# One more fold for the rows n of 2 mod 4 in sequences 1 to 7 of a fused Fourier-mixing and squared-ReLU kernel

## The chip, the cores and the metric

The kernel runs on one core of a Trainium2 chip. The metric is the device time of one execution in microseconds (us). The core's engines work beside each other and meet through semaphores: TensorE (PE in the profile, with its weight loads as PEld), VectorE (DVE), ScalarE (ACT), GpSimd (POOL) and SyncE (SP), which issues most DMA transfers. A group of 128 rows of on-chip memory is called 128 partitions; matmul results land in PSUM, everything else in SBUF.

## What is computed

```python
X = np.fft.fft(np.fft.fft(x, axis=1), axis=2).real   # x: (8, 3008, 256), float32
h = X.reshape(24064, 256) @ w_in                     # w_in: (256, 2048)
out = np.maximum(h, 0.0) ** 2 @ w_out                # w_out: (2048, 256)
```

So eight sequences of S = 3008 rows go through a two-dimensional Fourier transform, of which the real part is kept, and then through two dense layers with a squared ReLU between them. All of it is in float32.

## The kernel before

**The transform along the sequence.** The rows of x come to the kernel in groups of four: n, S - n, S/2 - n and S/2 + n, for n from 0 to S/4 = 752. Sums and differences of the four (the folds, on VectorE) leave two kinds of folded rows, kp = 0 and kp = 1, which feed the outputs k of even and of odd number. What is left is a product of a cosine or sine table with the folded rows. The rows n are split into classes, because a table row of an even n repeats itself with changed signs in the second half of its columns, and so needs only half of them:

- class 0: n of 0 mod 8, one tile of 95 rows, a quarter of the columns (94 or 95)
- class 1: n of 4 mod 8, one tile of 94 rows, 94 or 95 columns
- class 2: n of 2 mod 4 (the rows of the title), two tiles of 96 and 92 rows, half of the columns (188 or 189)
- class 3: the odd n, three tiles of 128, 128 and 120 rows, all columns (376 or 377)

The seven tiles are numbered t = 0 to 6, in this order: tiles 2 and 3 are class 2, and `ODD0` is tile 4.

For sequences 1 to 7 the odd rows (class 3) already get one fold more, n against S/4 - n. Tile 5 is loaded in reversed blocks of 32 rows, `f_turn` (L423; shuffle at L427 or L430, copy f0 at L433) reverses each block in turn, `f_even` (L443) makes the sum and the difference for kp = 0, `f_sine` (L448) multiplies by a sine on ScalarE, and `f_odd` (L452) combines by a cosine for kp = 1. Then `odd_n` (L549) needs half the columns for each product, 188 or 189, at L565. For kp = 1 the cosine and the sine part come out apart, side by side; ScalarE copies one to SBUF ("oc", L569) and `join_odd` (L572) adds and subtracts them into the columns of even and odd number. `part_table` (L325) sorts the columns of the tables of class 3 in place, once, before sequence 1.

**The groups of the transform.** Each sequence has four groups: `which` (0 for P, from the cosine tables, 1 for Q, from the sine tables) times kp. A group is five pieces: `even_n` (L494: four products, one each of classes 0 and 1 and two of class 2, through `product` at L475, whose matmul is at L487; then a copy on ScalarE, L502), `join_4`, `join_2`, `odd_n` and `join_1`. For kp = 1 `join_odd` comes between the last two. The joins run on VectorE. The even and odd products write to a ring of two PSUM buffers (psd).

**The dense layers.** A sequence is cut into six blocks of 251 (or 250) columns k, each block into eight steps j. A step has a `front` (L631) in two halves h: two products into PSUM buffer "ph" (L641, L642; a ring of two, so half h of a step needs what half h of the step before used), three VectorE operations that read it (L644, L646, L647), and after each half a call of `between`. ScalarE then applies ReLU and square (L656, L657), GpSimd makes four sums (L664 to L667), and two steps later `back` does seven products (L694). `gather` (L711 to L728) and the two transposing `store` parts (L758, L759) follow each block.

**What sets the order.** The engines run what the program emits, in that order. The folds and the transform of sequence b + 1 are done during the dense layers of sequence b. `ahead` (L766) lists them as pieces, each with a written weight, and `between` hands pieces out: each call lowers `spent` by `pace` (all weights over the number of calls, 78 in a sequence, 53 in the first), and pieces are emitted while `spent` is at or below zero, each raising it by its weight. After a tile of the odd class its `f_odd` is held back and put at the fourth place among the next tile's pieces. Sequence 0 is transformed ahead of all dense work, by the same helpers but without the further fold.

Of the kernel before, what the change touches and what calls it, by code (L numbers as in the profile page):

```python
# [8 lines left out]
F32 = mybir.dt.float32  # L9
# [4 lines left out]
P = 128  # L14
R = 32
# [67 lines left out]
def kernel(  # L83
# [12 lines left out]
    nc = tc.nc  # L96
    B, NROW, _, D = x.shape
    S = out.shape[0] // B
# [9 lines left out]
    TILES = class_tiles(S)  # L108
    NT = len(TILES)
    NC = column_counts(S)  # L110
    PLACE, WT = table_places(S)
# [3 lines left out]
    const = ctx.enter_context(tc.tile_pool(name="const", bufs=1))  # L115
    xp = ctx.enter_context(tc.tile_pool(name="xp", bufs=NX))
# [3 lines left out]
    hp = ctx.enter_context(tc.tile_pool(name="hp", bufs=3))  # L120
# [3 lines left out]
    op = ctx.enter_context(tc.tile_pool(name="op", bufs=2))  # L124
# [9 lines left out]
    xt = {}  # L134
# [3 lines left out]
    ODD0 = NT - 3  # L138
    HALF = S // 16
    REST = HALF - P  # L140
# [2 lines left out]
           [(0, P, H // 2)] + [(H // 2 + p, 2 * HALF - P - p - R, R) for p in range(0, H // 2, R)]]  # L143
    assert H == P and REST <= H // 2 and TILES[ODD0][0] == 3 and TILES[ODD0 + 1][1] == TILES[ODD0][1] + P

    def load_x(b, t):
        c, r0, step, rows = TILES[t]
        if b and c == 3:
            xt[b, t] = xp.tile([P, 4, D], F32, name="xt", tag="x")
            for p, first, count in ODD[t - ODD0]:  # L150
                nc.sync.dma_start(out=xt[b, t][p:p + count], in_=x[b, S // 8 + 1 + first:S // 8 + 1 + first + count])
            return

        while rows % 15 and rows % 16 and r0 + step * rows < NROW:
            rows += 1

        pool, tag = (gp, "g") if b == 0 and t < NT - NX else (xp, "x")
        xt[b, t] = pool.tile([P, 4, D], F32, name="xt", tag=tag)
        nc.sync.dma_start(out=xt[b, t][0:rows], in_=x[b, r0:r0 + step * (rows - 1) + 1:step])
# [3 lines left out]
    cosT = const.tile([P, 2, WT], F32, name="cosT")  # L163
# [147 lines left out]
    PQE = {}  # L311
    PART = (slice(0, H + 1), slice(H + 1, D))
    REVERSE = list(range(R - 1, -1, -1))
    turn = const.tile([P, 3, 2], F32, name="turn")

    def make_turn():
        for i in range(2):
            for a, tab in enumerate((cosT, sinT, sinT)):
                nc.scalar.mul(turn[:, a, i:i + 1], tab[:, 1, PLACE[ODD0 + i]:PLACE[ODD0 + i] + 1], -1.0 if a == 2 else 1.0)

    rows_used = const.tile([P, 1], F32, name="rows_used")
    nc.vector.memset(rows_used, 0.0)
    nc.vector.memset(rows_used[0:REST], 1.0)

    def part_table(tab, i):  # L325


        nk, at = NC[0][3], PLACE[ODD0 + i]
        v = tab[:, 0, at:at + nk]
        a = op.tile([P, nk], F32, name="tp", tag="os")  # L330
        nc.scalar.mul(a, v, rows_used if i else 1.0)
        nc.scalar.copy(v[:, 0:(nk + 1) // 2], a[:, 0::2])
        nc.scalar.copy(v[:, (nk + 1) // 2:], a[:, 1::2])

    def columns(tab, t, part):

        nk, at = NC[0][3], PLACE[t]
        nq = (nk + 1) // 2
        return tab[:, 0, at + part * nq:at + (nk if part else nq)]

# [21 lines left out]
    def fold(b, t):  # L362


        odd = b > 0 and t >= ODD0
        r = slice(0, P if odd else TILES[t][3])
        st = {}

        def new(pool, nm, shape):
# [30 lines left out]
        def w_of(t):  # L400
            if (b, t) not in folded:
                folded[b, t] = wp.tile([P, 2, D], F32, name="w", tag="w")
            return folded[b, t]
# [9 lines left out]
        if b == 0:  # L413
            return [f_s, f_d, f_sc, f_dc, lambda: (f_w(PART[0]), f_e()), lambda: f_w(PART[1])]
        ops = [(0.9, f_s), (0.9, f_d), (0.7, f_sc), (0.6, f_dc), (1.1, f_w)]
        if not odd or t == ODD0:
            return ops, None


        i = t - ODD0 - 1  # L420
        rows = slice(0, TILES[ODD0 + i][3] if i == 0 else REST)

        def f_turn():  # L423
            w = w_of(t)
            if i == 0:
                st["v"], st["w"] = w_of(ODD0), w
                nc.vector.stream_shuffle(w, w, REVERSE)  # L427
            else:
                st["v"], st["w"] = w, w_of(NT)
                nc.vector.stream_shuffle(st["w"][0:H // 2], w[H // 2:P], REVERSE)  # L430
                nc.gpsimd.memset(st["w"][H // 2:P], 0.0)
            spare("f0", "f0")
            nc.scalar.copy(st["f0"][rows], st["v"][rows, 0])  # L433
# [21 lines left out]
                nc.vector.scalar_tensor_tensor(out=u, in0=u, scalar=turn[rows, 0, i:i + 1], in1=st[nm][rows],  # L455
                                               op0=ALU.mult, op1=ALU.add)

        return ops + [(0.8, f_turn), (1.3, f_even), (0.2, f_sine)], (1.4, f_odd)

    def dft_ops(b):  # L460

# [6 lines left out]
        def group(kp, which):  # L468
# [6 lines left out]
            def product(ps, c, lone_e=False, only=None):  # L475

                ts = [t for t in range(NT) if TILES[t][0] == c]
                for t in ts if only is None else ts[only:only + 1]:
                    rows = TILES[t][3]
                    if b is None:  # L480
                        w = we[0:rows, kp, t, 0:n]
                    elif lone_e:
                        w = lone[0:rows, 2 * t + kp]
                    else:
                        w = folded[b, t][0:rows, kp, PART[which]]
                        w = w if which else w[:, 0:n]
                    nc.tensor.matmul(ps[0:w.shape[-1]], w,  # L487
                                     (cosT if lone_e else tab)[0:rows, kp, PLACE[t]:PLACE[t] + NC[kp][c]],
                                     start=t == ts[0] and (lone_e or not both_in), stop=t == ts[-1] and not lone_e,
                                     skip_group_check=both_in)  # L490
# [3 lines left out]
            def even_n():  # L494
                st["ps"] = psd.tile([P, 512], F32, name="pd", tag="d")[0:n]
                for c, at, nk in EVEN:
                    product(st["ps"][:, at:at + nk], c)
                copy_4()

            def copy_4():  # L500
# [36 lines left out]
            def join_2():  # L537
                a, ps = st["b"], st["ps"]
                st["c"] = hp.tile([P, NC[0][3]], F32, name="dc2", tag="dc2", bufs=2)[0:n, 0:n0]
                both(st["c"][:, 0:n1], st["c"][:, n1:n0], a, ps[:, 2 * n2:2 * n2 + n1])  # L540

            def odd_part(i, lone_e):

# [2 lines left out]
                    st["odd"] = pool.tile([P, 512], F32, name="pd", tag=tag)[:, 0:n0]  # L546
                product(st["odd"], 3, lone_e, i)

            def odd_n():  # L549
                ps = psd.tile([P, 512], F32, name="pd", tag="d")[0:n]  # L550
                st["odd"] = ps[:, 0:n0]
                if b is None:
                    return product(ps[:, 0:n0], 3)
                nq = (n0 + 2) // 2 if kp else (n0 + 1) // 2
                for part in range(2):
                    if kp:
                        tab, o = (cosT, sinT)[part], 0
                        to = ps[:, part * nq:part * nq + nq]
                        other = part != which
                    else:  # L560
                        tab, o = (cosT, sinT)[which], part
                        to = ps[:, part:n0:2]
                        other = part != which
                    for i, pair in enumerate(((ODD0, ODD0 + 1), (ODD0 + 2, NT))):
                        nc.tensor.matmul(to, folded[b, pair[other]][:, kp, PART[which]][:, 0:n],  # L565
                                         columns(tab, ODD0 + i, o), start=i == 0, stop=i == 1)
                if kp:
                    st["cos"] = hp.tile([P, nq], F32, name="oc", tag="oc", bufs=1)[0:n]
                    nc.scalar.copy(st["cos"], ps[:, 0:nq])  # L569
                    st["sin"] = ps[:, nq:2 * nq]  # L570

            def join_odd():  # L572

                a, ps = st["cos"], st["sin"]
                nq = a.shape[-1]
                st["odd"] = o = hp.tile([P, NC[1][3]], F32, name="do", tag="do", bufs=1)[0:n, 0:n0]
                tt(out=o[:, 0::2], in0=a[:, 0:nq - 1], in1=ps[:, 0:nq - 1], op=ALU.add)
                if which == 1:
                    tt(out=o[:, 1::2], in0=ps[:, 1:nq], in1=a[:, 1:nq], op=ALU.subtract)
                else:  # L580
                    tt(out=o[:, 1::2], in0=a[:, 1:nq], in1=ps[:, 1:nq], op=ALU.subtract)
# [19 lines left out]
                return [((which, kp, nm), f) for nm, f in named]  # L601
            ops = [(0.1, even_n), (0.4, join_4), (0.5, join_2), (0.1, odd_n), (0.8, join_1)]
            if b and kp:
                ops.insert(4, (0.5, join_odd))
            return ops

        ops = [] if b is None else [(0.0, start)]
# [158 lines left out]
    def ahead(b):  # L766
        start, *groups = dft_ops(b)
        if b == 1:

            tables = [(0.3, lambda tab=tab, i=i: part_table(tab, i)) for i in range(2) for tab in (cosT, sinT)]  # L770
            groups = [(1.5, fold_columns)] + dft_ops(None) + tables + groups
        groups.insert(0, start)

        pieces = []
        for ops, last in [fold(b, t) for t in range(NT)] + [(groups + [(0.0, lambda: load_e(b))], None)]:
            if held:
                ops.insert(3, held.pop())
            if last:
                held.append(last)
            pieces += ops  # L780
        return pieces
# [231 lines left out]
```

## Time and profile before

The median of three runs is 1944.14 us (1943.55 to 1944.79).

| engine | busy us | share of the span | instructions |
|---|---|---|---|
| PE (matmul) | 1930.5 | 99% | 9266 |
| PEld (weight load) | 1716.5 | 88% | 9266 |
| DVE | 1396.0 | 72% | 3432 |
| ACT | 924.9 | 48% | 1074 |
| POOL | 1172.9 | 60% | 1708 |

Busy time is the time in which an engine has at least one instruction under way. One float32 product shows as two matmul records, each with its own weight load. The durations of matmul records overlap (a record of 251 columns is shown as 375 ns, while the next starts 0.21 us after it), so what a product costs TensorE is read from the chain of waits, which shows start to start: 0.42 us for the two records of a product of 251 columns. The transform of sequences 1 to 7 is a small part of TensorE's time: in the chain L487 has 1.9% and L565 1.8%, while the four dense lines L641, L642 and L694 have nearly all the rest.

### The profile page before, as it was taken

Reading aid. Unit: us, or ns where it says so; the run is one execution under the profiler, and the core shown is the slowest. Engines: PE = TensorE matmul, PEld = TensorE weight load, DVE = VectorE, ACT = ScalarE, POOL = GpSimd, SP = SyncE. Lnnn points to the kernel's source line nnn. Section 1 sums busy time; section 2 is a strip of 40 time slices with the busy share of each in tenths; the row PEclk is TensorE's granted clock in tenths of the full one; section 3 lists DMA queues with packets and bytes.
Section 4 is the critical chain, followed back from the end, with each engine's and each line's share of the span. In section 5 each row is a group of like instructions: output and inputs, shape, how many; then the busy total and the mean of one; then the engine's idle time right before and its main releaser. Section 6 shows DMA issues by size and latency. Waiting matters only on the chain.

```text
span 1942.7 us, 27736 instructions
## 1 busy us (share of the span) xinstructions
PE 1930.5 (99%) x9266; PEld 1716.5 (88%) x9266; DVE 1396.0 (72%) x3432; ACT 924.9 (48%) x1074; POOL 1172.9 (60%) x1708
## 2 busy tenths in 40 slices
PE   9999999999999999999999999999999999999998
PEld 7888888888988899888988889888898888988887
DVE  8998866777677766777667776777766777655554
ACT  2854544544444444445444454444544454444443
POOL 0047646676567655766666665667656676556655
PEclk9999999999999999999999999999999999999999
DMA  7332101111111101121012100121012101100101
GB/s 216 114 36 53 38 10 49 33 31 27 27 41 32 37 12 30 39 41 28 11 35 43 40 20 12 41 48 28 20 17 52 33 12 22 27 12 12 22 11 22
DMA packets 145563, 69.55 MB, mean 36 GB/s; under 512 B 129090, under 2 KB 136204, under 8 KB 145419
## 3 DMA queue, kind: packets, MB, share of 16 engines
q1 hardware_dynamic: 144960, 66.86, 15.8%
q8 instruction: 73, 1.20, 0.3%
q14 instruction: 71, 0.58, 0.1%
q0 software_dynamic: 176, 0.65, 0.1%
q10 hardware_dynamic: 283, 0.26, 0.0%
HBM read 43.03 MB, written 24.69 MB: 35 GB/s over the span
## 4 chain that ended last, share of the span: by engine, by line
PE 95%; DVE 3%; DMA 1%; SPq 0%; issue 0%; ACT 0%; DVEq 0%
PE ph L642 17%; PE ph L641 16%; PE mC L694 16%; PE mA L694 16%; PE mB L694 16%; PE mD L694 8%; PE pd L487 2%; PE pd L565 2%; DMA raw<-in_moe_w_in_dram 1%; DVE m L263 0%; DMA xt<-in_x_dram 0%; DMA sind<-in_sin_d_dram 0%; DVE fd L261 0%; DVE he L644 0%; PE mA L681 0%
## 5 line engine op out<-in xcount | busy, mean ns | idle before, releaser
L656 ACT ACTIVATE g<-g 128x1004 f32<-128x1004 f32 (+1 forms) x384 | 399.3, 1040 | 792.5 <-DVE g L647 438.5
L644 DVE SCALAR_TENSOR_TENSOR he<-Et,gE,ph 128x251 f32<-128x251 f32 (+1 forms) x768 | 361.8, 471 | 412.5 <-PE ph L642 410.4
L664 POOL TENSOR_TENSOR s<-g 128x251 f32<-128x251 f32 (+1 forms) x376 | 246.4, 655 | 659.7 <-ACT g L657 584.7
L642 PE MATMUL ph<-Qt,G 127*128 127x251 f32 (+1 forms) x1536 | 451.9, 375 | 0.0
L641 PE MATMUL ph<-Pt,G 128*128 128x251 f32 (+1 forms) x1536 | 451.7, 375 | 0.0
L657 ACT ACTIVATE g<-g 128x1004 f32<-128x1004 f32 (+1 forms) x384 | 399.3, 1040 | 12.2
L694 PE MATMUL mC<-s,wsum 128*128 128x251 f32 (+1 forms) x1504 | 381.7, 375 | 0.0
L694 PE MATMUL mA<-g,wout 128*128 128x251 f32 (+1 forms) x1504 | 379.8, 374 | 0.0
L646 DVE TENSOR_TENSOR g<-he,ph 128x251 f32<-128x251 f32 (+1 forms) x768 | 320.5, 417 | 55.3 <-POOL s L664 1.4
L642 PEld LDWEIGHTS ph<-Qt,G 127*128 127x128 f32 x1536 | 291.5, 190 | 35.9
L641 PEld LDWEIGHTS ph<-Pt,G 128*128 128x128 f32 x1536 | 287.6, 189 | 35.5 <-DVE g L647 1.2
L694 PEld LDWEIGHTS mC<-s,wsum 128*128 128x128 f32 x1504 | 285.6, 190 | 34.7
L694 PEld LDWEIGHTS mA<-g,wout 128*128 128x128 f32 x1504 | 282.9, 189 | 36.0 <-issue 1.3
L647 DVE TENSOR_TENSOR g<-he,ph 128x251 f32<-128x251 f32 (+1 forms) x768 | 314.2, 409 | 0.0
L666 POOL TENSOR_TENSOR s<-g 128x251 f32<-128x251 f32 (+1 forms) x376 | 304.4, 810 | 0.0
L665 POOL TENSOR_TENSOR s<-s,g 128x251 f32<-128x251 f32 (+1 forms) x376 | 274.6, 730 | 29.5
L667 POOL TENSOR_TENSOR s<-g,s 128x251 f32<-128x251 f32 (+1 forms) x376 | 253.9, 675 | 0.0
L694 PE MATMUL mB<-g,wsum 128*128 128x251 f32 (+1 forms) x752 | 220.5, 374 | 0.0
L694 PE MATMUL mD<-s,wout 128*128 128x251 f32 (+1 forms) x752 | 220.3, 374 | 0.0
L694 PE MATMUL mB<-s,wout 128*128 128x251 f32 (+1 forms) x752 | 219.9, 374 | 0.0
L694 PEld LDWEIGHTS mB<-g,wsum 128*128 128x128 f32 x752 | 142.6, 190 | 17.4
L694 PEld LDWEIGHTS mD<-s,wout 128*128 128x128 f32 x752 | 141.9, 189 | 17.7
(136 smaller groups left out, 1304.4 us busy)
## 6 DMA issues: line engine op xcount, KB each, us to landing
out_dram<-os SPq DMA_DIRECT2D x376, 56.0 KB
xt<-in_x_dram SPq DMA_DIRECT2D x32, 384.0 KB
xt<-in_x_dram SPq DMA_DIRECT2D x42, 128.0 KB
Et<-e_dram SPq DMA_DIRECT2D x7, 752.5 KB
xt<-in_x_dram SPq DMA_DIRECT2D x9, 512.0 KB
out_dram<-os SPq DMA_DIRECT2D x288, 6.8 KB
raw<-in_moe_w_in_dram SPq DMA_DIRECT2D x16, 256.0 KB
raw<-in_moe_w_out_dram SPq DMA_DIRECT2D x16, 256.0 KB
```

Of the source, the lines that this page charges most:

```text
L641: nc.tensor.matmul(hP, G1[:, fs], pt[:, ks], start=True, stop=True)
L642: nc.tensor.matmul(hQ, G2[0:P - 1, fs], qt[0:P - 1, ks], start=True, stop=True)
L644: nc.vector.scalar_tensor_tensor(out=t, in0=et[:, ks], scalar=gE[:, fc:fc + 1], in1=hP, op0=ALU.mult, op1=ALU.add)
L646: tt(out=g[:, h, 0, 0:n], in0=t, in1=hQ, op=ALU.add)
L647: tt(out=g[:, h, 1, 0:n][:, ::-1], in0=t, in1=hQ, op=ALU.subtract)
L656: act(v, v, AF.Relu)
L657: act(v, v, AF.Square)
L664: gt(out=s1, in0=g21, in1=g22, op=ALU.add)
L665: gt(out=s2, in0=s1, in1=g11, op=ALU.subtract)
L666: gt(out=s3, in0=g11, in1=g21, op=ALU.subtract)
L667: gt(out=s4, in0=g12, in1=s2, op=ALU.subtract)
L694: nc.tensor.matmul(acc[nm][:, i, 0:n], w, v[:, 0:n], start=j == 0 and i == 0, stop=j == NJ - 1, skip_group_check=True)
```

## The change

In sequences 1 to 7 class 2 gets the further fold that class 3 already has. Its 188 rows are paired, first with last, so that 94 pairs are left; for each of these a sum and a difference are kept, each for half of the columns. The purpose is to stream fewer columns through TensorE: `even_n` still has two products of class 2 in each group, of 94 rows in place of 96 and 92, and of 94 or 95 columns in place of 188 or 189.

For that, tile 3 is loaded in three reversed blocks of 32 rows, and it gets the pieces turn, even, sine and odd, with weights of 0.8, 0.7, 0.2 and 1.2. `even_n` calls the new helper `once_more`, which holds what `odd_n` did before, and for kp = 1 a second `join_odd`, named "half" and weighted 0.4, comes ahead of `join_2`. It shares the buffers "oc" and "do" with the join of class 3. The tables of tile 2 are sorted as those of class 3 are, ahead of them, and `make_turn` takes three more columns of the tables.

The core of the diff:

```diff
+    TWO = ODD0 - 2
+    HALF2 = S // 32
+    ROWS2 = TILES[TWO][3]
...
+        if b and t == TWO + 1:
+            xt[b, t] = xp.tile([P, 4, D], F32, name="xt", tag="x")
+            for p in range(0, ROWS2, R):
+                at = TILES[TWO][1] + step * (2 * HALF2 - p - R)
+                nc.sync.dma_start(out=xt[b, t][p:p + R], in_=x[b, at:at + step * (R - 1) + 1:step])
+            return
...
-        odd = b > 0 and t >= ODD0
-        r = slice(0, P if odd else TILES[t][3])
+        odd, two = b > 0 and t >= ODD0, b > 0 and t == TWO + 1
+        r = slice(0, P if odd else ROWS2 if two else TILES[t][3])
...
-        i = t - ODD0 - 1
-        rows = slice(0, TILES[ODD0 + i][3] if i == 0 else REST)
+        i = 2 if two else t - ODD0 - 1
+        rows = slice(0, (P, REST, HALF2)[i])
...
-        return ops + [(0.8, f_turn), (1.3, f_even), (0.2, f_sine)], (1.4, f_odd)
+        return ops + [(0.8, f_turn), (1.3 if odd else 0.7, f_even), (0.2, f_sine)], (1.4 if odd else 1.2, f_odd)
...
                 for c, at, nk in EVEN:
-                    product(st["ps"][:, at:at + nk], c)
+                    if b and c == 2:
+                        st["half"] = once_more(st["ps"][:, at:], c, nk)
+                    else:
+                        product(st["ps"][:, at:at + nk], c)
                 copy_4()
...
-                both(st["c"][:, 0:n1], st["c"][:, n1:n0], a, ps[:, 2 * n2:2 * n2 + n1])
+                both(st["c"][:, 0:n1], st["c"][:, n1:n0], a, st["half"] if b else ps[:, 2 * n2:2 * n2 + n1])
...
+            def once_more(ps, c, nk):
+
+                nq = (nk + 2) // 2 if kp else (nk + 1) // 2
+                pairs, rows = ((((TWO, TWO + 1),), HALF2), (((ODD0, ODD0 + 1), (ODD0 + 2, NT)), P))[c == 3]
+                for part in range(2):
+                    if kp:
+                        tab, o = (cosT, sinT)[part], 0
+                        to = ps[:, part * nq:part * nq + nq]
+                    else:
+                        tab, o = (cosT, sinT)[which], part
+                        to = ps[:, part:nk:2]
+                    for i, pair in enumerate(pairs):
+                        nc.tensor.matmul(to, folded[b, pair[part != which]][0:rows, kp, PART[which]][:, 0:n],
+                                         columns(tab, pairs[0][i] if c == 3 else TWO, o)[0:rows],
+                                         start=i == 0, stop=i == len(pairs) - 1)
+                if not kp:
+                    return ps[:, 0:nk]
+                a = hp.tile([P, NC[0][3] // 2 + 1], F32, name="oc", tag="oc", bufs=1)[0:n, 0:nq]
+                nc.scalar.copy(a, ps[:, 0:nq])
+                return a, ps[:, nq:2 * nq]
...
             if b and kp:
-                ops.insert(4, (0.5, join_odd))
+                ops.insert(4, (0.5, lambda: join_odd("odd", n0)))
+                ops.insert(2, (0.4, lambda: join_odd("half", n1)))
...
-            tables = [(0.3, lambda tab=tab, i=i: part_table(tab, i)) for i in range(2) for tab in (cosT, sinT)]
+            tables = [(0.3, lambda tab=tab, t=t: part_table(tab, t)) for t in (TWO, ODD0, ODD0 + 1)
+                      for tab in (cosT, sinT)]
```

More of the change, by code (lines that the diff above doesn't have):

```diff
@@ L144 @@
     assert H == P and REST <= H // 2 and TILES[ODD0][0] == 3 and TILES[ODD0 + 1][1] == TILES[ODD0][1] + P
+    TWO = ODD0 - 2
+    HALF2 = S // 32
+    ROWS2 = TILES[TWO][3]
+    assert TILES[TWO][0] == TILES[TWO + 1][0] == 2 and HALF2 <= ROWS2 < HALF2 + R and ROWS2 % R == 0
     def load_x(b, t):
@@ L313 @@
     REVERSE = list(range(R - 1, -1, -1))
-    turn = const.tile([P, 3, 2], F32, name="turn")
+    turn = const.tile([P, 3, 3], F32, name="turn")
     def make_turn():
-        for i in range(2):
+        for i, t in enumerate((ODD0, ODD0 + 1, TWO)):
             for a, tab in enumerate((cosT, sinT, sinT)):
-                nc.scalar.mul(turn[:, a, i:i + 1], tab[:, 1, PLACE[ODD0 + i]:PLACE[ODD0 + i] + 1], -1.0 if a == 2 else 1.0)
+                r = slice(0, TILES[t][3])
+                nc.scalar.mul(turn[r, a, i:i + 1], tab[r, 1, PLACE[t]:PLACE[t] + 1], -1.0 if a == 2 else 1.0)
     rows_used = const.tile([P, 1], F32, name="rows_used")
@@ L323, with part_table @@
     nc.vector.memset(rows_used[0:REST], 1.0)
[L325 to L331, printed above, removed]
+    def part_table(tab, t):
+        nk, at = NC[0][TILES[t][0]], PLACE[t]
+        rows = TILES[t][3]
+        v = tab[0:rows, 0, at:at + nk]
+        a = op.tile([P, nk], F32, name="tp", tag="os")[0:rows]
+        nc.scalar.mul(a, v, rows_used if t == ODD0 + 1 else 1.0)
         nc.scalar.copy(v[:, 0:(nk + 1) // 2], a[:, 0::2])
@@ L335, in columns @@
     def columns(tab, t, part):
-        nk, at = NC[0][3], PLACE[t]
+        nk, at = NC[0][TILES[t][0]], PLACE[t]
         nq = (nk + 1) // 2
@@ L415, in fold @@
         ops = [(0.9, f_s), (0.9, f_d), (0.7, f_sc), (0.6, f_dc), (1.1, f_w)]
-        if not odd or t == ODD0:
+        if not (odd or two) or t == ODD0:
             return ops, None
-        i = t - ODD0 - 1
-        rows = slice(0, TILES[ODD0 + i][3] if i == 0 else REST)
+        i = 2 if two else t - ODD0 - 1
+        rows = slice(0, (P, REST, HALF2)[i])
         def f_turn():
             w = w_of(t)
-            if i == 0:
-                st["v"], st["w"] = w_of(ODD0), w
-                nc.vector.stream_shuffle(w, w, REVERSE)
+            if i != 1:
+                st["v"], st["w"] = w_of(t - 1), w
+                nc.vector.stream_shuffle(w[r], w[r], REVERSE)
             else:
@@ L553, in odd_n, with join_odd @@
                     return product(ps[:, 0:n0], 3)
[L554 to L574, printed above, removed]
+                st["odd"] = once_more(ps, 3, n0)
+            def join_odd(what, nk):
+                a, ps = st[what]
                 nq = a.shape[-1]
-                st["odd"] = o = hp.tile([P, NC[1][3]], F32, name="do", tag="do", bufs=1)[0:n, 0:n0]
+                st[what] = o = hp.tile([P, NC[1][3]], F32, name="do", tag="do", bufs=1)[0:n, 0:nk]
                 tt(out=o[:, 0::2], in0=a[:, 0:nq - 1], in1=ps[:, 0:nq - 1], op=ALU.add)
```

## The prediction

> **What bounds the kernel now.** I read the page's totals first, then the chain that ended last, then the waits, and last the stretches that the change touches.
>
> ```profile
> span 1942.7 us, 27736 instructions
> PE 1930.5 (99%) x9266; PEld 1716.5 (88%) x9266; DVE 1396.0 (72%) x3432; ACT 924.9 (48%) x1074; POOL 1172.9 (60%) x1708
> ...
> PE 95%; DVE 3%; DMA 1%; SPq 0%; issue 0%; ACT 0%; DVEq 0%
> ```
>
> TensorE is busy for 99% of the span, and it makes up 95% of the chain; the 3% of VectorE and 1% of DMA lie in the opening, which the change leaves alone. Two stretches of the windows view, one late in the first sequence and one across the middle ones, tell how much room VectorE has (columns: stretch, length, busy time of PE, PEld, DVE, ACT, POOL with instructions in brackets, clock, DMA share, GB/s):
>
> ```profile
> 120.00:240.00 120.00, 120.00 (x564) 104.48 (x563) 106.56 (x254) 58.61 (x68) 82.99 (x117) 1.00 0.26 45
> 290.00:1700.00 1410.00, 1410.00 (x6756) 1260.80 (x6755) 1016.34 (x2484) 665.11 (x746) 909.15 (x1310) 1.00 0.14 31
> ```
>
> TensorE has no gap in either. VectorE is at 72% in the middle but at 89% in the first sequence, where the folding of sequence 1 is squeezed into fewer steps. The waits agree (waiting group, releaser, total us, times, longest):
>
> ```profile
> DVE he L644 <- PE ph L642: 410.4, 322, 3.6
> ...
> PEld ph L641 <- DVE g L647: 1.2, 5, 0.4
> ```
>
> VectorE waits for TensorE; the reverse is 1.2 us of weight loads in the whole run. So time taken off TensorE shortens the run, as long as VectorE's added work does not make TensorE wait.
>
> The chain around two of the transform's bursts (start, us, what; each f32 product shows as two matmul records, so x8 is four products):
>
> ```profile
> 701.03 0.42 PE ph L642 x2
> 701.45 1.09 PE pd L487 x8
> 702.55 0.42 PE ph L641 x2
> ...
> 711.47 0.43 PE ph L642 x2
> 711.89 1.28 PE pd L565 x8
> 713.17 0.42 PE ph L641 x2
> ```
>
> L487 is even_n: records of 95, 95, 94, 94 columns (two of each class, classes 0 and 1) and four of 189 (class 2, its two row tiles). L565 is odd_n: eight records of 188 or 189.
>
> **What the Trainium skill says.** (1) "TensorE: Matmul & The Clock Gate", section "LDWEIGHTS (loading the stationary operand)": a weight load takes its columns divided by 1.2 in ns, whatever its rows; 128 columns give 106.7 ns, and section "Back-to-back issue gap" says that load and matmul together set the spacing. The trace agrees on both counts: loads of 128 columns take the same time from 92 or 96 rows, and the slope is (191 - 88) ns over 121 columns, 0.85 ns a column.
>
> ```profile
> L487 PEld LDWEIGHTS pd<-cosT,w 92*128 92x128 f32 x32 | 5.6, 191 | 0.0
> L487 PEld LDWEIGHTS pd<-cosT,w 96*128 96x128 f32 x32 | 4.9, 191 | 0.0
> L487 PEld LDWEIGHTS pd<-cosT,we 128*7 128x7 f32 x8 | 0.5, 88 | 1.6 <-issue 1.2 <-DVE db L530 0.3
> ```
>
> (2) "SBUF — State Buffer", section "Who interferes with whom": a VectorE instruction with two SBUF inputs contends with a GpSimd instruction that reads SBUF, and the loser waits for all of the other. The trace fits: the same 128x256 addition is 742 ns at L445, and of one shape at L408 the means run from 414 to 945 ns by tile.
>
> **The change, part by part.**
>
> *Removed: columns on TensorE.* In even_n of sequences 1 to 7, class 2 had two products of 188 or 189 columns, one for each row tile. It gets two products again, of 94 rows and 94 or 95 columns. Count: 7 sequences x 4 groups = 28 bursts, each with four records that shrink. A long record costs 1.28/8 = 160 ns (L565 burst). A short one costs (1.09 - 4 x 0.160)/4 = 112 ns (L487 burst). That is not half: 95 columns would stream in about 80 ns by the long record's rate, so a short record is set by its weight load, as the skill's 106.7 ns says. Saved per burst: 4 x (160 - 112) = 0.19 us; with the load's 106.7 ns, 0.21 us. Over 28 bursts: 5.4 us (low end) to 6.0 us (high end). I take **5.5 us**, since the 112 ns is measured in place. A burst then is 8 x 112 = 0.90 us. The interleaved PSUM columns of kp = 0 cost nothing: odd_n writes that way at kp = 0, contiguously at kp = 1, and both bursts take 1.28 us.
>
> *Added: VectorE.* The nearest rows are those of the odd class:
>
> ```profile
> L446 DVE TENSOR_TENSOR w<-f,w 128x256 f32<-128x256 f32 x6 | 4.4, 736 | 0.2
> L427 DVE STREAM_SHUFFLE w<-w 128x512 f32<-128x512 f32 x6 | 4.4, 731 | 0.0
> L445 DVE TENSOR_TENSOR w<-f,w 128x256 f32<-128x256 f32 x6 | 4.5, 742 | 0.0
> L455 DVE SCALAR_TENSOR_TENSOR w<-w,turn,f 128x256 f32<-128x256 f32 x12 | 7.5, 666 | 0.0
> L577 DVE TENSOR_TENSOR do<-oc,pd 128x188 f32<-128x188 f32 x6 | 2.1, 351 | 1.8 <-ACT oc L569 1.8
> ```
>
> Rows do not matter (60-row forms of L446 take the same 736 ns). Per sequence: shuffle 0.73, f_even 0.74 + 0.74, f_odd 2 x 0.67, join of "half" in two groups, 4 x 0.35 = 1.40; together 4.95 us, 35 us over seven sequences. It lies beside TensorE: VectorE goes from 1396 to about 1431 us, 74% of the span; in the middle sequences it still idles 27% of the time, and that idle time hides it.
>
> *Added: ScalarE.* The copy f0, four sine multiplications and two "oc" copies, at 388, 387 and 318 ns: 2.6 us a sequence, 18 us in all, plus two more sorted tables and three multiplications of one column once. ScalarE is busy 48%. The "oc" copy comes ahead of copy_4's copy, so join_4, which waits for that copy, starts up to 0.32 us later in half of the groups, and the next half-step's three VectorE operations queue behind it. TensorE needs what they free only a step (4.7 us) later, so this costs nothing.
>
> *Moved: one tile's load.* One transfer of 96 rows becomes three of 32, with the same bytes, issued three tiles ahead while the DMA share is 0.14. Nothing.
>
> *Moved: the first even_n of sequence 1* now needs sorted class-2 tables. They come first of six tables, four tables ahead of the burst. Between 0 and 1 us, once; I take 0.
>
> *The pacing.* between() hands out pieces by their written weights: 45.4 for a middle sequence over 78 calls before, 49.1 after; for sequence 1, 51.9 over 53 calls before, 56.2 after. All later pieces shift. What matters is which fall together, because TensorE's lead is thin in places:
>
> ```profile
> 338.03 1.82 DVE L408 TENSOR_TENSOR w<-sc 94x256 f32<-94x256 f32 x2
> ...
> 340.61 0.41 DVE L647 TENSOR_TENSOR g<-he,ph 128x251 f32<-128x251 f32 x1
> ```
>
> ```profile
> 341.24 0.59 PE L641 MATMUL ph<-Pt,G 128*128 128x251 f32 x2
> ```
>
> The L408 pair, put between the halves of a step, lets the second half's psh buffer go at 340.61 + 0.41 = 341.02, and TensorE writes it at 341.24: 0.22 us to spare. That is the heaviest neighbourhood: f_dc and f_w (0.5 + 1.8 us) in two calls running. I walked through the weights call by call. In the middle sequences the new pieces' worst neighbours are turn and even of tile 3 in the two halves of one step, 0.73 + 1.48 = 2.2 us, no heavier than that; f_w keeps its neighbour f_dc. So 0 there. In the first sequence, f_dc with f_w of tile 3 (one call), then turn, even, sine with f_s, f_d follow each other: 2.3 + 0.7 + 1.5 + 0.8 + 0.8 = 6.1 us of pieces in two steps, beside 2 x 2.35 us of the steps' own, 10.8 us against 9.4 us. That runs over by 1.4 us, of which a lead of about 2 us hides most. Bounds: 0 to 3 us, once; I take 0.5.
>
> Sum: 1944.14 - 5.5 + 0.5 = **1939.1 us**.
>
> **The rivals.**
>
> *A, the first sequence stalls more.* For it: VectorE's 89% there, and almost one piece a call. Against it: no TensorE gap at all in that stretch now. Two or three overruns of about 1 us: 1944.1 - 5.5 + 3 = 1941.6.
>
> *B, the short products are no cheaper.* If eight short records in a row fall back to the weight load's 190 ns, or two loads cannot overlap so often, the gain is nil: 1944. Against it: four in a row run at 112 ns now.
>
> *C, VectorE becomes the bound in spots, slower.* If f_even and f_odd of tile 3 each land next to a heavy piece in every sequence, with 0.22 us to spare, each stalls TensorE by its length less that: 1.26 + 1.12 = 2.4 us, 17 us over seven: 1944.1 - 5.5 + 17 = 1955.6. For it: the 0.22 us, and the doubling by GpSimd contention that stretches such pieces. Against it: my walk through the weights, and the 27% idle time.
>
> **How the numbers follow.** Main forecast 0.70 (1939.1), A 0.16, B 0.06, C 0.08. Faster by over 0.2% means under 1940.3: the main case and a third of A, 0.75. Same: the rest of A and B, 0.17. Slower: C, 0.08. The range starts at the high end of the gain with no stall (1938.1, with the run's own scatter of 0.6 us: 1937.5) and takes in A: 1942.6.
>
> **What would show it.** Right: the class-2 even bursts at 0.9 us in the chain instead of 1.09; odd bursts still 1.28; TensorE's matmul count unchanged at about 9266; its busy time shorter by about 5 us; VectorE near 1430 us; no new TensorE wait in the middle sequences. Wrong: bursts that stay near 1.09 us (B), waits of PE or PEld for DVE g L647 (C), or such waits only before 290 us (A).

## The result and the profile after

The changed kernel takes 1938.53 us (median of six runs, 1938.12 to 1940.64) against 1944.25 us before (six runs beside it); the ratio is 0.9972 with a 95% interval of 0.9959 to 0.9985. So it is faster by 0.28%, 5.7 us; 1939.1 us was forecast. In the changed kernel the lines have moved: `even_n`'s products of classes 0 and 1 are at L501, those of `once_more` (class 2 and class 3) at L578, the front's at L664 and L665, its VectorE operations at L667, L669 and L670, and `back` at L717.

The totals and the shares of the chain, from the page after:

```profile
span 1936.3 us, 27908 instructions
PE 1924.3 (99%) x9266; PEld 1711.0 (88%) x9266; DVE 1424.3 (74%) x3502; ACT 939.0 (48%) x1132; POOL 1184.1 (61%) x1708
...
PE 95%; DVE 4%; DMA 0%; issue 0%; ACT 0%; DVEq 0%; SPq 0%
```

The number of matmul records is the same, 9266, and their busy time is 6.2 us shorter. VectorE has 28.3 us more, and the run does not feel it. The two stretches of the windows view, and the waits that tell who waits for whom:

```profile
120.00:240.00 120.00, 119.81 (x562) 103.92 (x560) 107.11 (x258) 60.18 (x73) 83.54 (x116) 1.00 0.24 45
290.00:1700.00 1410.00, 1410.00 (x6780) 1260.99 (x6779) 1043.57 (x2548) 679.17 (x792) 921.88 (x1314) 1.00 0.11 31
```

```profile
DVE he L667 <- PE ph L665: 382.5, 303, 3.4
...
PEld ph L664 <- DVE g L670: 1.0, 2, 0.6
```

TensorE still has no gap in the middle stretch. In the first sequence it has one, of 0.2 us. VectorE's waiting for TensorE shrank from 410 to 383 us, by about as much as its busy time grew: that is where its added work went.

The chain around the bursts of the same groups as before:

```profile
699.07 0.43 PE ph L665 x2
699.49 0.42 PE pd L501 x4
699.91 0.45 PE pd L578 x4
700.36 0.45 PE ph L664 x2
...
709.73 1.28 PE pd L578 x8
```

The even burst is now 0.42 + 0.45 us long where it was 1.09, and the front's product behind it shows 0.45 in place of 0.42, since the weight load of its second record starts 0.03 us behind the first record, where else such a load starts with it. Counted from the start of the last record ahead of a burst to the start of the second record behind it, less the 0.42 us that two such records cost, the even bursts average 1.096 us before and 0.897 us after: 0.199 us each, 5.57 us over 28. The odd burst is unchanged at 1.28 us.

A second measure is used below: the length of a middle sequence, from the first matmul of its first front to that of the next sequence, read from the start times in the trace. Neighbouring sequences differ by up to 0.05 us, so the means are given; these repeat to 0.01 us from one pair of sequences to the next. The measure leaves out the opening, whose end lies anywhere from 42.6 to 44.4 us in these runs. Before it is 233.80 us, after 232.95 us. Of the 0.85 us, four bursts make up 0.80.

### The profile page after: what moved, and what is told of

It is laid out like the page before. It is cut to its first block, busy times and chain, and to the rows that moved or that the text cites. A ratio compares the mean times of both kernels' runs of the same rounds, so it can differ in the third digit from the quotient of the medians.

```text
span 1936.3 us, 27908 instructions
## 1 busy us (share of the span) xinstructions
PE 1924.3 (99%) x9266; PEld 1711.0 (88%) x9266; DVE 1424.3 (74%) x3502; ACT 939.0 (48%) x1132; POOL 1184.1 (61%) x1708
## 4 chain that ended last, share of the span: by engine, by line
PE 95%; DVE 4%; DMA 0%; issue 0%; ACT 0%; DVEq 0%; SPq 0%
PE ph L664 17%; PE ph L665 17%; PE mC L717 16%; PE mA L717 16%; PE mB L717 16%; PE mD L717 8%; PE pd L578 2%; PE pd L501 1%; DVE m L274 0%; DVE w L422 0%; DVE he L667 0%; DVE fd L272 0%; PE mA L704 0%; PE mB L704 0%; DVE g L670 0%
## 5 line engine op out<-in xcount | busy, mean ns | idle before, releaser
L667 DVE SCALAR_TENSOR_TENSOR he<-Et,gE,ph 128x251 f32<-128x251 f32 (+1 forms) x768 | 361.8, 471 | 385.7 <-PE ph L665 382.5
L664 PE MATMUL ph<-Pt,G 128*128 128x251 f32 (+1 forms) x1536 | 452.5, 375 | 0.2 <-DVE g L670 0.2
L665 PE MATMUL ph<-Qt,G 127*128 127x251 f32 (+1 forms) x1536 | 452.2, 375 | 0.0
L717 PE MATMUL mC<-s,wsum 128*128 128x251 f32 (+1 forms) x1504 | 381.4, 374 | 0.0
L717 PE MATMUL mA<-g,wout 128*128 128x251 f32 (+1 forms) x1504 | 379.9, 374 | 0.0
L669 DVE TENSOR_TENSOR g<-he,ph 128x251 f32<-128x251 f32 (+1 forms) x768 | 320.6, 418 | 54.5 <-DVE he L667 0.9
L665 PEld LDWEIGHTS ph<-Qt,G 127*128 127x128 f32 x1536 | 291.8, 190 | 35.9
L664 PEld LDWEIGHTS ph<-Pt,G 128*128 128x128 f32 x1536 | 287.0, 189 | 36.3 <-DVE dc L547 1.3
L717 PEld LDWEIGHTS mC<-s,wsum 128*128 128x128 f32 x1504 | 285.5, 190 | 34.5
L670 DVE TENSOR_TENSOR g<-he,ph 128x251 f32<-128x251 f32 (+1 forms) x768 | 314.5, 409 | 0.0
L717 PEld LDWEIGHTS mA<-g,wout 128*128 128x128 f32 x1504 | 282.6, 189 | 35.0 <-issue 0.3
L688 POOL TENSOR_TENSOR s<-s,g 128x251 f32<-128x251 f32 (+1 forms) x376 | 279.6, 744 | 29.5
L690 POOL TENSOR_TENSOR s<-g,s 128x251 f32<-128x251 f32 (+1 forms) x376 | 260.2, 692 | 0.0
L717 PE MATMUL mB<-g,wsum 128*128 128x251 f32 (+1 forms) x752 | 220.5, 374 | 0.0
L717 PE MATMUL mD<-s,wout 128*128 128x251 f32 (+1 forms) x752 | 220.3, 374 | 0.0
L717 PE MATMUL mB<-s,wout 128*128 128x251 f32 (+1 forms) x752 | 219.9, 374 | 0.0
L717 PEld LDWEIGHTS mB<-g,wsum 128*128 128x128 f32 x752 | 142.5, 190 | 17.5
L717 PEld LDWEIGHTS mD<-s,wout 128*128 128x128 f32 x752 | 141.9, 189 | 17.7
```

The lines of the kernel that those rows point to most:

```text
L664: nc.tensor.matmul(hP, G1[:, fs], pt[:, ks], start=True, stop=True)
L665: nc.tensor.matmul(hQ, G2[0:P - 1, fs], qt[0:P - 1, ks], start=True, stop=True)
L667: nc.vector.scalar_tensor_tensor(out=t, in0=et[:, ks], scalar=gE[:, fc:fc + 1], in1=hP, op0=ALU.mult, op1=ALU.add)
L669: tt(out=g[:, h, 0, 0:n], in0=t, in1=hQ, op=ALU.add)
L670: tt(out=g[:, h, 1, 0:n][:, ::-1], in0=t, in1=hQ, op=ALU.subtract)
L688: gt(out=s2, in0=s1, in1=g11, op=ALU.subtract)
```

## The experiments

The kernels ran in groups, each on one chip and beside the kernel before, whose own median differs a little from group to group; so the ratios are to be compared, and not the medians alone.

| kernel | median us | ratio to before (95%) | middle sequence us |
|---|---|---|---|
| before | 1944.25 to 1945.11 by group | 1 | 233.80 |
| changed | 1938.53 | 0.9972 (0.9959 to 0.9985) | 232.95 |
| short_only | 1938.80 | 0.9972 (0.9961 to 0.9982) | 232.95 |
| vector_only | 1945.31 | 1.0002 (0.9994 to 1.0011) | 233.74 |
| true_weights | 1939.87 | 0.9975 (0.9965 to 0.9984) | 232.95 |
| even_twice | 1940.18 | 0.9974 (0.9964 to 0.9984) | 232.95 |
| even_four_times | 1958.49 | 1.0071 (1.0056 to 1.0086) | 235.2, twice 236.9 |
| add_128_48 | 1960.26 | 1.0081 (1.0066 to 1.0096) | 235.87 |
| add_64_48 | 1960.62 | 1.0079 (1.0064 to 1.0094) | 235.87 |
| add_64_94 | 1962.82 | 1.0094 (1.0077 to 1.0111) | 236.29 |
| first_128_48 | 1951.48 | 1.0035 (1.0022 to 1.0049) | 234.74 |
| first_128_94 | 1952.93 | 1.0040 (1.0026 to 1.0054) | 234.74 |
| first_64_48 | 1954.15 | 1.0048 (1.0033 to 1.0063) | 235.18 |

**The two halves of the change apart.** Theory 1 is the prediction's: TensorE's records set the time and VectorE's work is hidden. Theory 2: the short products save more than is seen, and the added VectorE work gives part of it back.

short_only takes the added pieces of VectorE and ScalarE away:

```diff
-        odd, two = b > 0 and t >= ODD0, b > 0 and t == TWO + 1
+        odd, two = b > 0 and t >= ODD0, False
...
-                if not kp:
+                if not kp or c == 2:
                     return ps[:, 0:nk]
...
-                ops.insert(2, (0.4, lambda: join_odd("half", n1)))
```

> Only the TensorE half of the change: even_n has the short products of class 2, but tile 3 gets no turn, even, sine and odd, and the class-2 columns are not joined a second time (left out: that part of the fold, so the output differs). Theory 1 (28 bursts with four records of 112 instead of 160 ns, and VectorE's added work hidden): as the changed kernel, 1938.5, or up to 0.5 us less. Theory 2 (the added VectorE work costs TensorE time and the short products save more than is seen): below 1937. VectorE's busy time back near 1396 us, even bursts 0.86 us in both.

vector_only keeps them and puts the long products back:

```diff
-                        st["half"] = once_more(st["ps"][:, at:], c, nk)
+                        product(st["ps"][:, at:at + nk], c)
+                        st["half"] = apart(st["ps"][:, at:at + nk], nk)
```

(`apart` is the end of `once_more`, the "oc" copy and the two parts.)

> Only the VectorE and ScalarE half: all added folds, copies and joins stay, but even_n has the two long products of class 2 of the kernel before (left out: the short products; the output differs). Theory 1: as the kernel before, 1944.2, up to 0.5 us more; even bursts 1.09 us, VectorE near 1424 us, no new waits of TensorE in the middle sequences. Theory 2: 1946 or more.

Measured for short_only: 1938.80 us, the changed kernel's ratio, and a middle sequence of 232.95 us, the same as the changed kernel's, with VectorE at 1392.5 us. For vector_only: 1945.31 us, a ratio of 1.0002, with VectorE at 1424.1 us. The chain of vector_only, with the long burst back:

```profile
702.53 1.09 PE pd L501 x8
```

What follows: the whole gain is in the short products, and the VectorE half by itself costs nothing in the middle sequences. In the first sequence it costs 0.25 us in the trace (260.04 against 259.79 us), which the totals are too coarse to tell. Theory 2 falls: without that work a middle sequence is not even 0.01 us shorter.

**What a short record costs.** The prediction read 112 ns from the chain and put it down to the weight load. Two more products in each even_n test that by their widths: 4 records in 28 bursts.

```diff
                     else:
                         product(st["ps"][:, at:at + nk], c)
+                if b:
+                    for t in (TWO, TWO + 1):
+                        nc.tensor.matmul(st["ps"][0:min(n, 128), 400:448], folded[b, t][0:HALF2, kp, 0:min(n, 128)],
+                                         columns(cosT, TWO, 0)[0:HALF2, 0:48], start=True, stop=True)
                 copy_4()
```

> The changed kernel with two more products in each even_n of sequences 1 to 7, of 128 (or 127) weight columns and 48 moving columns, to unused columns of the same PSUM buffer: 4 records in 28 bursts. Theory 1 (a short record is set by its weight load, 111 ns whatever it streams): 28 x 4 x 0.111 = 12.4 us more, 1951. Rival (it streams: 48 columns at 0.84 ns are 40 ns): 4.5 us more, 1943.

> The same two added products with 64 weight columns and 48 moving columns. Theory 1 (load of 64 columns, 0.85 ns a column, 54 ns, is longer than the 40 ns of streaming): 28 x 4 x 0.054 = 6.0 us more, 1944.6. If an added record costs a fixed 111 ns whatever its weights: 1951.

> The same two added products with 64 weight columns and 94 moving columns. Theory 1 (the longer of load and streaming: 54 against 79 ns): 28 x 4 x 0.079 = 8.9 us more, 1947.4. If the load alone sets it: 6.0 us, 1944.6. If fixed: 1951.

All three missed by far, at 1960 to 1963 us; no theory had that. The waits of add_128_48 show why (waiting group, releaser, total us, times, longest):

```profile
PEld pd L517 <- ACT oc L588: 6.9, 14, 0.5
PE pd L517 <- ACT oc L588: 4.6, 14, 0.3
```

In the 14 groups of kp = 1, `once_more` has already emitted ScalarE's "oc" copy from that PSUM buffer, and the added product, which writes the same buffer, waits for it: there the burst takes 1.90 us, and in the groups of kp = 0, which have no such copy, 1.34 us. That was a flaw of the experiment, not a property of short products. So the same products went ahead of even_n's own, where nobody has read the buffer yet:

```diff
+                if b:
+                    for t in (TWO, TWO + 1):
+                        nc.tensor.matmul(st["ps"][0:min(n, 128), 400:448], folded[b, t][0:HALF2, kp, 0:min(n, 128)],
+                                         columns(cosT, TWO, 0)[0:HALF2, 0:48], start=True, stop=True)
                 for c, at, nk in EVEN:
```

> The changed kernel with the two added products of 128 (or 127) weight columns and 48 moving columns ahead of even_n's own, so that no added product follows the reading of the buffer by ScalarE (that wait of about 0.5 us in 14 bursts is what I found in the earlier three). Theory 1 (weight load sets a short record, 111 ns): 28 x 4 x 0.111 = 12.4 us more than the changed kernel, 1951. Rival (streaming, 40 ns): 4.5 us more, 1943.

> The same with 94 moving columns, the width of the change's own short products. Theory 1: the same 111 ns a record, 12.4 us more, 1951, within 0.5 us of the 48-column run. Rival (streaming, 79 ns): 8.9 us more, 1947.4, and 4.4 us above the 48-column run.

> The same with 64 weight columns and 48 moving columns. Theory 1: 54 to 58 ns a record, 6.5 us, and twice about 0.1 us a burst where the weights' width changes, as the earlier runs showed, 5 us: 1949 to 1950. If the load of 128 columns has nothing to do with the 111 ns: 1951.

Measured: 1951.48 and 1952.93 us. These totals are 1.45 us apart where at most 0.5 was expected, but the difference lies outside the bursts (in the profiled runs 0.3 us in the opening and 1.3 us after the last matmul): a middle sequence takes 234.74 us in both, 1.79 us more than the changed kernel's, which over 16 added records is 112 ns. The chain of first_128_48, and then of first_128_94:

```profile
703.50 0.38 PE pd L512 x4
703.88 0.49 PE pd L501 x4
704.37 0.45 PE pd L582 x4
704.81 0.45 PE ph L668 x2
```

```profile
703.79 0.42 PE pd L512 x4
704.21 0.45 PE pd L501 x4
704.66 0.45 PE pd L582 x4
705.11 0.45 PE ph L668 x2
```

Half the columns make L512 shorter by 0.04 us (its first record only), and the next group longer by as much: from 703.50 to 704.81 and from 703.79 to 705.11 it is 1.31 and 1.32 us. Streaming is ruled out as what sets a record of 48 to 94 columns under 128 weight columns.

With 64 weight columns the records follow one another 58 ns apart for 48 moving columns (first_64_48) and 81 ns apart for 94 (add_64_94). That fits the longer of load and streaming, 54 and 79 ns by the expectations' estimates, so the 112 ns goes with the number of weight columns. But the total of first_64_48 missed: 1954.15 us, above both of its theories (1949 to 1950, and 1951). The change between 128 and 64 weight columns costs more than I had put in: a burst is 0.551 us longer than the changed kernel's, of which four records at 58 ns are 0.232, so that the two changes of width take 0.32 us. The trace shows what differs there. Between records of one width the next weight load starts with the record before it; the load of the first narrow record starts only with its own record (703.652 and 703.653 us), and so does that of the first wide one behind them (704.013 and 704.015 us). With the weights the rows of the output change too, from 128 to 64, and which of the two holds the load back these runs do not tell. Narrow weights in the midst of wide ones are no gain at all here: a middle sequence is 0.44 us longer than with wide ones of the same columns.

**How much more VectorE work there is room for.** Two and then six more additions were put ahead of f_even's two for tile 3, in the same piece:

```diff
+            for _ in range(2 if two else 0):
+                tt(out=st["more"][rows], in0=a, in1=w, op=ALU.add)
             tt(out=v, in0=a, in1=w, op=ALU.add)
```

> The changed kernel with two more 94x256 additions ahead of f_even's two for tile 3, in the same piece, to a spare buffer: about 1.5 us more VectorE work in one place per sequence, so that the piece is 2.8 us long. Theory 1 (TensorE's lead over VectorE is about 2 us there and hides what fits): a loss of 0 to 0.7 us a sequence, 1938.5 to 1943.5, with waits of TensorE for DVE g only at that place. Rival (26% idle time hides anything): 1938.5 with no such wait.

> The changed kernel with six more 94x256 additions ahead of f_even's two for tile 3: one piece of about 5.7 us per sequence, 4.4 us more VectorE work. Theory 1 (a lead of about 2 us is all that hides it): 3 to 4 us of waits a sequence, 1960 to 1966. Rival (idle time over the sequence hides it): 1938.5 to 1940.

Measured: with two, a middle sequence of 232.95 us, no change, and TensorE's waits for VectorE's g are those of the changed kernel; the total of 1940.18 us (1938.36 to 1941.96) has the changed kernel's ratio within its interval. Both theories allow that, so this run alone does not tell them apart. With six, 1958.49 us. The trace of that kernel, VectorE first, then TensorE:

```profile
379.54 4.18 DVE L462 TENSOR_TENSOR more<-f,w 94x256 f32<-94x256 f32 x6
383.65 0.94 DVE L463 TENSOR_TENSOR w<-f,w 94x256 f32<-94x256 f32 x1
384.62 0.74 DVE L464 TENSOR_TENSOR w<-f,w 94x256 f32<-94x256 f32 x1
...
386.18 0.41 DVE L674 TENSOR_TENSOR g<-he,ph 128x251 f32<-128x251 f32 x1
```

```profile
384.37 0.59 PE L721 MATMUL mD<-s,wout 128*128 128x251 f32 x2
386.65 0.69 PE L668 MATMUL ph<-Pt,G 128*128 128x251 f32 x2 [1.69 <-DVE g L674]
```

The piece holds VectorE from 379.54 to about 385.3, so the "ph" buffer that TensorE needs next comes free only at 386.18 + 0.41 = 386.59, and TensorE starts at 386.65 after 1.69 us of idleness. A sequence with such a stall takes 2.3 us more than the changed kernel's (this product costs some 1.96 us of it, and the same product of the step's second half, also late, the other 0.31), and VectorE has 4.4 us more to do: the lead there hides about 2.1 us, and the 26% of idle time in the rest of the sequence hides nothing of what is left. Below the expected 1960 to 1966, but of the kind that theory 1 named: it is the lead at the spot that counts.

**The written weights.**

```diff
-        return ops + [(0.8, f_turn), (1.3 if odd else 0.7, f_even), (0.2, f_sine)], (1.4 if odd else 1.2, f_odd)
+        return ops + [(0.8, f_turn), (1.3, f_even), (0.2, f_sine)], (1.4, f_odd)
```

> The changed kernel with the written weights of tile 3's pieces set to those of the odd tiles (even 1.3 for 0.7, odd 1.4 for 1.2), so that between() spreads them as their durations ask. Theory 1 (lead suffices, one stall of 0.2 us in the first sequence): 1938.2 to 1938.7, the stall gone or moved. Rival (where pieces fall together matters): off by 1 us or more either way.

Measured: 1939.87 us (1938.86 to 1941.41), a ratio of 0.9975 whose interval overlaps the changed kernel's. The middle sequences are the same to 0.01 us; the first takes 260.03 us against 259.29, and the start times there account for it. In the changed kernel the front's products start late at one place, by 0.46 us (188.9 us in the trace); here they do at three (193.8, 203.8 and 213.4 us), by 1.19 us together. Weights nearer to the durations are no better; where the pieces fall in the crowded first sequence decides, by less than 1 us.

No version from these runs beats the changed kernel.

## Why the prediction was right, point by point

- **The gain per burst** was put at 0.19 to 0.21 us and 5.5 us in all. Measured: 0.199 us, 5.57 us in 28 bursts. The reading behind it, that a record of 95 columns costs its weight load, was then shown by first_128_48 and first_128_94 (112 ns for 48 columns and for 94) and by first_64_48 (58 ns with half of the weight columns). "TensorE: Matmul & The Clock Gate" of the Trainium skill, section "LDWEIGHTS (loading the stationary operand)", gives 106.7 ns for 128 columns; the measured spacing is 5 ns above it.
- **VectorE's added work** was put at 35 us and "hidden". Hidden is shown by short_only and vector_only in the middle sequences. The durations of the added records sum to 30.5 us in seven sequences, 4.4 us in each in place of 4.95. Two terms were too large: the join of "half", costed with the row of 188 columns at 0.35 us where it has 94, and f_even, whose first addition takes 0.48 us in place of 0.74, while its second takes 0.83:

```profile
L460 DVE TENSOR_TENSOR w<-f,w 94x256 f32<-94x256 f32 x6 | 5.0, 830 | 0.2
...
L459 DVE TENSOR_TENSOR w<-f,w 94x256 f32<-94x256 f32 x6 | 2.9, 475 | 0.0
...
L599 DVE TENSOR_TENSOR do<-oc,pd 127x94 f32<-127x94 f32 x6 | 1.5, 247 | 0.0
```

  The times of f_even's two additions go with GpSimd's sums. With no such sum beside it an addition takes 0.41 us (at 173.21 us of the trace); in the middle sequences it ends 0.28 us after the sum that was running when it began, which has 0.2 us left when the first addition begins and 0.55 when the second does. The page's 28.3 us is another count: it takes the time in which two records overlap only once. Summed record by record, VectorE has 35.6 us more, the added 30.5 and 5.1 in pieces that were there before.
- **That the idle time hides it** was the wrong half of the reason (and by the prediction's own figures it is 26%, not 27%). even_four_times has VectorE at 74% of the span too, and stalls in every middle sequence. What held is the other half, the walk through the pieces, by which no neighbourhood there becomes heavier than TensorE's lead.
- **ScalarE's added work** was put at 18 us. Summed record by record it is 16.9 us in seven sequences, and 19.3 with the tables and the columns that are made once; the page has 14.1, again with overlaps counted once. The "oc" copy of 95 columns is 0.24 us, not 0.32. It costs the middle sequences no time, as said.
- **The first sequence's stall** was put at 0.5 us, bounded by 0 and 3. Its size was right and its place was not, so that part is luck. The first sequence is shorter by 0.50 us (259.79 to 259.29) where four bursts save 0.80, so 0.3 us is lost there. VectorE and then TensorE show where:

```profile
185.28 0.75 DVE L408 TENSOR_TENSOR sc<-fs 128x258 f32<-128x258 f32 x1
185.95 1.70 DVE L469 SCALAR_TENSOR_TENSOR w<-w,turn,f 94x256 f32<-94x256 f32 x2
...
188.41 0.41 DVE L670 TENSOR_TENSOR g<-he,ph 128x251 f32<-128x251 f32 x1
```

```profile
188.87 0.69 PE L664 MATMUL ph<-Pt,G 128*128 128x251 f32 x2 [0.19 <-DVE g L670]
```

  The walk named turn, even and sine of tile 3 beside f_s and f_d. It is f_odd of tile 3 (L469, 1.70 us where 1.34 was put in) behind f_sc of the next tile. TensorE's two records start 0.35 and 0.10 us late, 0.46 us in all; the kernel before has 0.15 us of this kind, at 165.8 us, which leaves the 0.3. vector_only has the same stall, behind the same two pieces. short_only does not have it, but its first sequence is no shorter (259.34 us): with the pieces handed out otherwise, f_dc and f_w of tile 3 fall together and TensorE starts late behind them, at 176.3 us.
- **The lead of about 2 us** that was to hide the pieces: at f_even of tile 3 in the middle sequences it hides 1.3 us more whole (even_twice) and about 2.1 us of 4.4 (even_four_times).
- **Rival B** fell with the bursts at 0.9 us, **rival C** with middle sequences that have no wait of TensorE for VectorE. C's mechanism is real, as even_four_times shows, but at that place it needs a piece of more than 2.6 us (even_twice's, without cost), twice what the change puts there. **Rival A** is there with 0.3 us in place of 3.
- **The total** came within 0.6 us of the forecast. That says less than the bursts do, since the opening alone ends up to 1.8 us earlier or later from run to run.

What stays open: 0.05 us of the 0.85 us by which each middle sequence shrank lies outside the bursts, and vector_only has it too (233.74 against 233.80).

## What to carry to other kernels

When TensorE is the chain, price an edit in matmul records as they follow one another in the chain, and look for the floor: with 128 weight columns a float32 record here takes 112 ns whether it streams 48 or 95 columns, so halving 189 columns saves 30%, and halving once more would save nothing. Work added to another engine is hidden up to the lead that TensorE has at that spot, not up to the engine's idle time: compare the longest piece in one place with the lead there. The engine's share of busy time does not tell: at 74% of the span, 1.3 us more in one place cost nothing and 4.4 us cost 2.3. The busy time of two profiles tells added work only roughly, since it counts overlapping records once. In an experiment that adds work to a buffer, look first at who has been set to read the buffer by then.

## What had not been expected of the hardware

A stall of TensorE can cost more than itself. In even_four_times, after the 1.69 us wait, the granted clock fell to half for 3.4 us, from 388.07 to 391.48 us; the windows view shows it (columns as above; clock third from the end):

```profile
384.00:386.60 2.60, 0.95 (x5) 0.51 (x3) 2.46 (x6) 1.15 (x4) 1.08 (x2) 1.00 0.00 0
...
388.00:391.40 3.40, 3.40 (x9) 2.75 (x9) 2.70 (x7) 2.00 (x3) 1.26 (x2) 0.51 0.00 0
```

Records of 251 columns then followed one another 0.42 us apart in place of 0.21, and that sequence took 236.9 us where the others with the same stall took 235.2. It happened in two of the six middle sequences; the other four, whose stalls are as long (1.69 to 1.71 us), had no such sequel. In the other twelve traces the clock never falls between 60 us and the last 4 us. In each trace all changes of the clock lie whole multiples of 3.413 us apart. On that grid the two stalls with a sequel began 0.30 and 0.53 us into an interval, and the four without one 0.83 to 1.69 us into it, all six ending within it. So where a stall falls on the grid goes with what follows it; six cases are few, and why it is so stays open.

And a change of the weights' width from 128 to 64 columns and back costs some 0.32 us in a burst, as first_64_48 showed.
